# Other places for X copies, transposes, routing pieces, weight halves and the last chunks in attention

## The chip, the cores and the metric

The kernel runs on one core of a Trainium2 chip. The metric is device time in microseconds (us) from start to end of the program. Three runs of the kernel before took 641.72, 642.62 and 643.10 us (median 642.62). A fourth execution was profiled: all rows in this document come from it.

The engines are PE (TensorE, matrix products), DVE (VectorE), ACT (ScalarE), POOL (GpSimd) and SP (which issues most transfers). Each works through its own list of instructions in order; an instruction waits until those of other engines that it depends on are done, and everything behind it on its engine waits too.

## What is computed

An attention with a causal window of 128 and a bias by distance, and behind it a mixture of experts that sends each token to one of 8 experts:

```
scores = scale * q @ k.T
scores = where(mask, scores + bias, -1e9)
attn = softmax(scores)
x = (attn @ v), heads side by side           # (4608 tokens, 512)
expert_idx = argmax(x @ w_gate)
out = gate_w * (relu(x @ w1[e]) @ w2[e])     # e = expert_idx of the token
```

Batch 8, 8 heads, sequence 576, head dimension 64; experts have 1024 hidden columns. All of it is 32-bit floating point.

## The kernel before

**Attention** goes over 36 chunks of 128 queries (all 8 heads of each). The work of a chunk `ch` is cut into pieces with one-letter names. On PE: `S00 S01 S10 S11`, the scores of head groups 0 and 1 (`scores`, L196 bias and L201 products, into the PSUM tiles `s_ps[0]` and `s_ps[1]`); `T`, the transposes of the exponentials (L236, into `t_ps`); `V U W Z`, the products with v (`values`, L277, into `r_ps`); `R`, `rows` (L299), which turns the result into token rows and gate logits and writes `t_ps` again. On DVE: `N0 N1` (`peak`, L211 and L213: fold and maximum), `X` (`copy_x`, L289: `r_ps` to `xT`), `I` (`invert`, L304), `Y` (`scale_rows`, L309, reads `t_ps`; then L1365 sums the logits). On ACT: `E0 E1` (`exps`, L222, eight exponentials), `P` (`place`, L244: `t_ps` to `pT`; POOL then does four selects on it, L247 and L250).

So `t_ps` goes round: `T` writes it, `P` empties it, `R` writes it, `Y` empties it, then the next `T`. `s_ps[0]` and `s_ps[1]` go round between scores, `N` and `E`. Most chunks are paired (`super_chunks`): two chunks share one `r_ps`, so the first product `V` of a pair waits until the `X` of both chunks of the pair before is done.

**The order by hand.** `PLACES`, `places` and `END` give each piece a step (relative to 4 times its chunk) and a rank in the step. `step(s)` sorts what falls in step s by rank and emits it; each engine keeps that order for the 147 steps. A *cycle* here is four steps: one `S10 S11`, one `T`, one `S00 S01`, half a pair's products, one `R`.

Into the same table other work is woven. *Routing pieces*: after every group of 5, 6, 3 or 5 chunks (`GROUPS`), `route` finds each token's expert and rank. It is a generator; each `yield` ends a piece, and `pieces` runs the next piece of every waiting group. For the groups that begin at chunks 0, 5, 10, 15 and 21 some of the small operations are on POOL (`eng`), the rest on DVE. Piece 1 is the maximum (L567); piece 2 `mk`, `oh` and `prev` (L582 to L586); piece 3 the rank products on PE (L590 to L594) and `pick` and its sums (L596 to L608); piece 4 the gates and POOL's `p`, `c`, `big` (L626 to L636); piece 5 `lp` and `eq` (L619, L643); piece 6 `rr` (L649, two instructions); piece 7 a product on PE and its sum into `base` (L655, L657). *Weight halves*: `round_half` (ACT, L1152) and `rest_half` (POOL, L1157) split a 128 x 512 half of an expert weight into two parts; `load_half` loads it. *Q scaling* (`scale_q`, POOL, L110). *Early expert work* (`EP`): two gathered tiles are transposed (`p0`, `p1`, L791), and the first layer of expert 0 is done for the first 256 of its tokens (`0` to `6`, L834, `LE` gives those done inside `route_last`).

`requests` issues the loads on SP that are due (`paced`). After the last chunk, `route_last` finishes the routing; its `idx` lets POOL gather the other rows of expert 0 (L782). Then the **experts** run on PE almost without a gap to the end (L834 first layer, L1040 second layer).

The lines at which the order is made:

```
n, i = divmod(s - 4 * W0 - at, 4 * W1)
todo.append((HOOKS["G"], 0, lambda: pieces(lambda c: c not in PACE and s % 4 == 3)))
for _, _, f in sorted(todo, key=lambda x: x[:2]):
    f()
```

Of the kernel before, what the change touches and what calls it, by code (L numbers as in the profile page):

```python
# [52 lines left out]
def attention(ctx, tc, st, qT, kT, v, iw, load_c2, chunk_done, chunks, begun):  # L53
# [326 lines left out]
    def step(s):  # L380
# [11 lines left out]
        for name, f in (("round", 0), ("rest_of", 3)):
            at, rank = HOOKS[name]
            n, i = divmod(s - 4 * W0 - at, 4 * W1)
            if i == 0 and 0 <= n < 14:
                todo.append((rank, 0, lambda name=name, n=n: st[name](n // 2, n % 2)))
# [33 lines left out]
ASIDE = (31, 33, 35)  # L430
ASIDE_X = (33, 34)
END = {0: dict(V=(7, 1), U=(7, 3), X=(8, 0.5), R=(10, 1), I=(10, 4), Y=(11, 2)),
       1: dict(V=(10, 0.9), U=(11, 3), X=(12, 0.5), R=(14, 1), I=(14, 4), Y=(15, 2)),
       30: dict(R=(22, 2.5), I=(22, 2.6), Y=(22, 3.2)),
       31: dict(R=(19, 3), I=(19, 3.1), Y=(19, 3.2)),
       32: dict(X=(15, 1), R=(16, 3), I=(16, 3.1), Y=(16, 3.2)),
       33: dict(V=(9, 3.5), U=(9, 3.6), W=(10, 3), Z=(10, 3.1), X=(11, 1.1), R=(13, 1), I=(13, 1.1), Y=(13, 1.2)),
       34: dict(V=(8, 1), U=(8, 1.1), X=(8, 2), R=(9, 3), I=(9, 3.1), Y=(9, 3.2)),
       35: dict(T=(3, 2), P=(3, 2.5), V=(6, 1), U=(6, 1.1), X=(6, 2), R=(6, 3), I=(6, 3.1), Y=(6, 3.2))}

# [995 lines left out]
```

## Time and profile before

| what | us |
|---|---|
| median of three runs (lowest, highest) | 642.62 (641.72, 643.10) |
| the profiled execution | 641.88 |
| its span (first to last instruction) | 639.80 |
| PE busy in the span | 590.5 (92%) |
| DVE, ACT, POOL busy | 379.7, 297.1, 319.7 |

Times in all rows count from the start of the span; the profiled execution has 2.08 us around it. Busy shares are means over stages that differ: until about 215 us attention uses all four engines, behind it PE alone is near full. A wait is the idle time of an engine just ahead of an instruction, put down to what ended it.

### The profile page before, as it was taken

The page shows a single profiled execution, that of the slowest core. Times are in us where ns is not written, and L with a number is a line of the kernel's source. Part 1 is how long each engine was busy: PE and PEld are TensorE (multiplying, and loading weights), DVE is VectorE, ACT ScalarE, POOL GpSimd, SP SyncE. Part 2 cuts the span into 40 slices and gives each one's busy share as a digit, 9 for nine tenths or more (in the row PEclk, how much of TensorE's full clock was granted, in tenths as well). Part 3 has the DMA queues.
Part 4 walks back from the last instruction along what each step waited for, and adds up shares of the span by engine and source line. Part 5 has one row for each costly group of instructions (what it writes and reads, how often), then busy time and mean ns, then how long its engine had stood idle before and what let it go on. Part 6 is the DMA issues. An engine that isn't in the chain of part 4 may idle for free.

```text
span 639.8 us, 18460 instructions
## 1 busy us (share of the span) xinstructions
PE 590.5 (92%) x7406; PEld 510.0 (80%) x7406; DVE 379.7 (59%) x914; ACT 297.1 (46%) x893; POOL 319.7 (50%) x484
## 2 busy tenths in 40 slices
PE   7879788889767889999999999999999999999996
PEld 5767666767656768989889999899899998888884
DVE  3757878888968767545553564465465456356411
ACT  5978878778644214433342343334333333333311
POOL 5667968867863031066417615742760760570202
PEclk9999999999889999999999999999999999999999
DMA  7768768768442263573525325433543542544201
GB/s 246 251 201 278 228 212 248 240 207 262 137 143 76 86 202 102 183 253 109 197 92 189 111 86 174 130 99 116 170 113 103 169 123 92 176 129 135 71 1 62
DMA packets 46907, 99.23 MB, mean 155 GB/s; under 512 B 12053, under 2 KB 13077, under 8 KB 46818
## 3 DMA queue, kind: packets, MB, share of 16 engines
q1 hardware_dynamic: 38194, 76.80, 37.3%
q0 software_dynamic: 8336, 20.96, 11.4%
q8 instruction: 59, 0.97, 0.6%
q10 hardware_dynamic: 288, 0.26, 0.1%
q14 instruction: 30, 0.25, 0.1%
HBM read 77.91 MB, written 20.09 MB: 153 GB/s over the span
## 4 chain that ended last, share of the span: by engine, by line
PE 64%; DVE 1%; DMA 1%; ACT 0%; POOLq 0%; issue 0%; POOL 0%; DVEq 0%
PE y_ps L1040 31%; PE l_ps L834 30%; PE s_ps L834 1%; PE x_ps L791 1%; DMA xg<-xd,idx 1%; PE y_ps L999 1%; PE x_ps L999 0%; ACT pT L839 0%; POOLq L1204 0%; ACT e_hh L837 0%; DVE y L1048 0%; PE s_ps L299 0%; DVE xT L289 0%; ACT l_ex L703 0%; DVE e_hl L840 0%
## 5 line engine op out<-in xcount | busy, mean ns | idle before, releaser
L837 ACT ACTIVATE hh<-l_ps 128x320 fp32r<-128x320 f32 (+4 forms) x104 | 46.5, 448 | 199.3 <-PE l_ps L834 199.3
L841 DVE SCALAR_TENSOR_TENSOR hl<-l_ps,hh 128x320 fp32r<-128x320 f32 (+4 forms) x104 | 52.2, 502 | 145.8 <-ACT hh L837 145.6
L814 POOL DMA_INDIRECT xg<-xd,od_idx x112 | 118.0, 1053 | 35.0 <-issue 32.5
L222 ACT ACTIVATE pe<-s_ps,nmax 128x128 f32<-128x128 f32 x288 | 102.2, 383 | 22.8 <-DVE nmax L213 7.9
L1040 PE MATMUL y_ps<-wh,hh 128*128 128x512 f32 x280 | 109.9, 392 | 0.0
L1040 PE MATMUL y_ps<-wl,hh 128*128 128x512 f32 x280 | 109.3, 390 | 0.0
L1040 PE MATMUL y_ps<-wh,hl 128*128 128x512 f32 x280 | 109.2, 390 | 0.0
L1028 POOL DMA_INDIRECT out<-y,od_pidx x33 | 34.5, 1044 | 146.5 <-ACT y L1046 140.0
L1140 DVE TENSOR_TENSOR wl<-w_raw,wh 128x512 fp32r<-128x512 f32 x114 | 73.8, 689 | 31.5 <-ACT wh L1136 31.2
L834 PE MATMUL l_ps<-xh,wh 128*128 128x320 f32 (+8 forms) x416 | 81.0, 316 | 0.0
L834 PE MATMUL l_ps<-xl,wh 128*128 128x320 f32 (+8 forms) x416 | 80.4, 315 | 0.0
L834 PE MATMUL l_ps<-xh,wl 128*128 128x320 f32 (+8 forms) x416 | 80.3, 315 | 0.0
L834 PEld LDWEIGHTS l_ps<-xh,wh 128*128 128x128 f32 x416 | 67.8, 188 | 6.7 <-issue 1.2
L277 PE MATMUL r_ps<-pT,v_sb 64*64 64x64 f32 (+2 forms) x1728 | 58.8, 264 | 9.8 <-DVE xT L289 6.2
L834 PEld LDWEIGHTS l_ps<-xl,wh 128*128 128x128 f32 x416 | 65.9, 188 | 2.0
L834 PEld LDWEIGHTS l_ps<-xh,wl 128*128 128x128 f32 x416 | 65.8, 188 | 2.0
L222 ACT ACTIVATION_READ_ACCUMULATOR pe<-s_ps,nmax 128x1 f32 x288 | 63.6, 221 | 0.0
L201 PE MATMUL s_ps<-k_sb,q_sb 64*64 64x192 f32 (+2 forms) x1152 | 61.8, 319 | 1.1 <-issue 1.1
L1136 ACT CAST wh<-w_raw 128x1024 fp32r<-128x1024 f32 x57 | 59.5, 1044 | 5.3 <-DMA w_raw<-w 5.3
L1040 PEld LDWEIGHTS y_ps<-wh,hl 128*128 128x128 f32 x280 | 52.6, 188 | 11.5
L1040 PEld LDWEIGHTS y_ps<-wh,hh 128*128 128x128 f32 x280 | 52.6, 188 | 9.7 <-ACT hh L837 0.4
L1040 PEld LDWEIGHTS y_ps<-wl,hh 128*128 128x128 f32 x280 | 52.6, 188 | 9.1
(236 smaller groups left out, 871.7 us busy)
## 6 DMA issues: line engine op xcount, KB each, us to landing
w_raw<-w SPq DMA_DIRECT2D x56, 512.0 KB, 3.8
v_sb<-v SPq DMA_DIRECT2D x36, 256.0 KB, 3.8
xd<-x_sb SPq DMA_DIRECT2D x32, 288.0 KB, 2.7
q_sb<-qT SPq DMA_DIRECT2D x35, 256.0 KB, 3.8
k_sb<-kT SPq DMA_DIRECT2D x23, 256.0 KB, 3.3
w_raw<-w SPq DMA_DIRECT2D x16, 256.0 KB, 3.7
w_n<-w SPq DMA_DIRECT2D x4, 1024.0 KB, 5.6
k_sb<-kT SPq DMA_DIRECT2D x8, 384.0 KB, 4.0
```

The source lines that it names most:

```text
L201: anchor(nc.tensor.matmul(out=heads[half(a), c, n, 64 * u0:].rearrange("q (u x) -> q u x", x=64), lhsT=blocks["q", ch][half(c), 2 * g + n, ...
L222: nc.scalar.activation(out=pes[ch][:, 2 * g + n, :, c, :], in_=s_ps[g][:, c, 192 * n + 64:192 * n + 192].rearrange("q (u x) -> q u x", x=6 ...
L277: anchor(nc.tensor.matmul(out=tops[half(p % 2), c, p // 2, i:i + n, :], lhsT=blocks["v", j][half(c), r, p, :], rhs=diagonal(pTs[group], ha ...
L791: nc.tensor.transpose(out=x_ps[:, d, :], in_=g[:, SUB * d + E:SUB * d + E + 128], identity=st["ident"])
L814: ins = tc.nc.gpsimd.indirect_dma_start(out=g[:, s], out_offset=None, in_=parts, in_offset=bass.IndirectOffsetOnAxis(ap=idx[:, s], axis=0),)
L834: nc.tensor.matmul(out=ps, lhsT=a[:, 128 * d:128 * d + 128], rhs=b[:, d], start=(k == 0), stop=(k == 11))
L837: nc.scalar.activation(out=hh, in_=ps, func=AF.Relu)
L841: nc.vector.scalar_tensor_tensor(out=hl, in0=ps, scalar=0.0, in1=hh.bitcast(F32), op0=ALU.max, op1=ALU.subtract)
L1028: ins = nc.gpsimd.indirect_dma_start(**kw).ins
L1040: nc.tensor.matmul(out=ys[t], lhsT=a[:, tl], rhs=b[:, 512:1024], start=(f == 0 and k == 0), stop=(f == 7 and k == 2))
L1136: keep(tc, nc.scalar.copy(out=wh, in_=raw))
L1140: keep(tc, eng.tensor_tensor(out=wl[:, sl], in0=raw[:, sl], in1=wh.bitcast(F32)[:, sl], op=ALU.subtract))
```

## The change

The places are other numbers. In words:

- `X` of the first chunk of a pair goes from the start of step 20 to the end of step 19; `X` of the second from behind `N1` of the running chunk to ahead of it (rank 2.5 to 0.3). `V` of a second chunk goes from step 10 (ahead of `R`) to step 11 (behind `R`, next to `U`).
- `T` goes from the end of step 4 to the start of step 5, `N0` behind `I`, `W` of some chunks ahead of `T` and `Z` behind it.
- Routing pieces run at the start of every third step of a cycle, ahead of `R`, `E1`, `I` and `N0`; before, they ran in the fourth step, ahead of `Y`. `prev` is on DVE in every group.
- Weight halves come every 9 steps from step 22 to 139 (before: every 8, from 20 to 124), at varying ranks. The loads get due times to match, and no load is placed later than step 148 (before: 140). Q is scaled one step earlier.
- The last chunks (30 to 35) have new places; `X` of chunk 32 goes to ACT too. Both early transposes `p0 p1` run in step 142, first layer `3` in step 146, `4 5` ahead of the last rank, `6` behind the last index products (before: `3 4`, then `5 6` between rank and index products).

```diff
-        if ch in ASIDE_X:
+        if ch in X_ACT:
...
-        at = min(due, PN * 35)
+        at = min(due, PN * 37)
...
-        ahead.setdefault(max(0, 4 * ch - 11), []).append(ch)
+        ahead.setdefault(max(0, 4 * ch - QAT[0]), []).append(ch)
...
-        todo.append((HOOKS["G"], 0, lambda: pieces(lambda c: c not in PACE and s % 4 == 3)))
+        for m, rank in PIECES:
+            if s % 4 == m:
+                todo.append((rank, 0, lambda: pieces(lambda c: c not in PACE)))
...
-PLACES = dict(S10=(0, 1), S11=(0, 2), E0=(0, 3), T=(4, 4), N1=(1, 2), P=(5, 3), S00=(-3, 5), S01=(-3, 6),
-              R=(22, 1), E1=(2, 2), N0=(-2, 3), I=(22, 4), Y=(23, 2))
+PLACES = {'S10': (0, 1), 'S11': (0, 2), 'E0': (0, 3), 'T': (5, 0.7), 'N1': (1, 2), 'P': (5, 3), 'S00': (-3, 5), 'S01': (-3, 6), 'R': (22, 1), 'E1': (2, 2), 'N0': (-2, 8), 'I': (22, 4), 'Y': (23, 2)}
...
+FIRST = {'X': (19, 5.5)}
+SECOND = {'V': (11, 2.5), 'U': (11, 3), 'W': (14, 0.9), 'Z': (15, 3), 'X': (17, 0.3)}
...
+PIECES = ((2, 0.5),)
...
-        at.update(X=(20, 0.5))
...
-        at.update(V=(10, 0.9), U=(11, 3), W=(14, 0.9), Z=(15, 3), X=(17, 2.5))
...
-EP = {0: ((30, "z"),), 52: ((30, "o"),), 131: ((30, "g"),), 142: ((2.3, "p0"),), 143: ((3.5, "p1"),), 144: ((2.5, "0"),), 145: ((2, "1"),), 146: ((2.5, "2"),)}
-LE = ("34", "56", "")
+EP = {0: ((30, 'z'),), 52: ((30, 'o'),), 131: ((30, 'g'),), 146: ((2.5, '2'), (3.53, '3')), 144: ((3.3, '0'),), 142: ((8, 'p0'), (8, 'p1')), 145: ((5.5, '1'),)}
+LE = ('45', '', '6')
...
-    eng.tensor_copy(out=prev, in_=run[:, c0, :])
+    nc.vector.tensor_copy(out=prev, in_=run[:, c0, :])
```

Three places in the instruction lists show what moved. The changed file is 11 lines shorter there, so L1365 reads L1354, L649 reads L638 and so on.

On DVE, around chunks 11 and 12, before: `Y` and its sum (L309, L1365), `X` (L289), `N1` (L211, L213), the second `X`, `N0`, `I` (L304), pieces 7 and 2 of two groups, then the next `Y`.

```order
L309 TENSOR_TENSOR x_sb<-t_ps,rinv 128x576
L1365 TENSOR_REDUCE lg<-x_sb 128x8
L289 COPY xT<-r_ps 128x512
L211 COPY_PREDICATED s_ps<-mask_sb,s_ps 128x2x2x64
L213 TENSOR_REDUCE nmax<-s_ps 128x4
L289 COPY xT<-r_ps 128x512
L211 COPY_PREDICATED s_ps<-mask_sb,s_ps 128x2x2x64
L213 TENSOR_REDUCE nmax<-s_ps 128x4
L304 RECIPROCAL rinv<-rsum 128x8
L657 TENSOR_TENSOR base<-base,s_ps 128x48
L582 TENSOR_REDUCE mk<-key 128x5
L584 TENSOR_TENSOR oh<-key,mk 128x40
```

The same place of the changed kernel:

```order
L309 TENSOR_TENSOR x_sb<-t_ps,rinv 128x576
L1354 TENSOR_REDUCE lg<-x_sb 128x8
L289 COPY xT<-r_ps 128x512 x2
L211 COPY_PREDICATED s_ps<-mask_sb,s_ps 128x2x2x64
L213 TENSOR_REDUCE nmax<-s_ps 128x4
L646 TENSOR_TENSOR base<-base,s_ps 128x48
L571 TENSOR_REDUCE mk<-key 128x5
L573 TENSOR_TENSOR oh<-key,mk 128x40
L575 CAST prev<-run 128x8
L304 RECIPROCAL rinv<-rsum 128x8
L211 COPY_PREDICATED s_ps<-mask_sb,s_ps 128x2x2x64
L213 TENSOR_REDUCE nmax<-s_ps 128x4
```

Both `X` now stand ahead of `N1`, and the pieces stand between `N1` and `N0` instead of between `N0` and `Y`.

On PE, the end of `S00 S01`, then `V` of chunk 10, `R` of chunk 7 and `U`, before:

```order
L201 MATMUL s_ps<-k_sb,q_sb 64x192 x8
L277 MATMUL r_ps<-pT,v_sb 64x128 x8
L277 MATMUL r_ps<-pT,v_sb 64x64 x8
L299 MATMUL t_ps<-iw_sb,xT 64x72 x16
L277 MATMUL r_ps<-pT,v_sb 64x128 x8
L277 MATMUL r_ps<-pT,v_sb 64x64 x8
```

And changed:

```order
L201 MATMUL s_ps<-k_sb,q_sb 64x192 x8
L299 MATMUL t_ps<-iw_sb,xT 64x72 x16
L277 MATMUL r_ps<-pT,v_sb 64x128 x8
L277 MATMUL r_ps<-pT,v_sb 64x64 x8
L277 MATMUL r_ps<-pT,v_sb 64x128 x8
L277 MATMUL r_ps<-pT,v_sb 64x64 x8
```

`R` now runs ahead of `V`, which is the instruction that waits for the two `X`.

On PE, the last routing (L710, L711 the rank of the last chunk, L834 the first layer, three rows each for `4`, `5` and `6`, L655 the first of the index products), before:

```order
L834 MATMUL s_ps<-e_xl,wh 128x256 x4
L710 LDWEIGHTS tri
L710 MATMUL t_ps<-l_oh,tri 128x8
L711 LDWEIGHTS tri
L711 MATMUL t_ps<-l_prev,tri 128x8
L834 MATMUL s_ps<-e_xh,wh 128x256 x4
L834 MATMUL s_ps<-e_xh,wl 128x256 x4
L834 MATMUL s_ps<-e_xl,wh 128x256 x4
L834 MATMUL s_ps<-e_xh,wh 128x256 x4
L834 MATMUL s_ps<-e_xh,wl 128x256 x4
L834 MATMUL s_ps<-e_xl,wh 128x256 x4
L655 LDWEIGHTS lp
```

And changed (L823 is the first layer, L699 and L700 the rank, L644 the index products):

```order
L823 MATMUL s_ps<-e_xh,wh 128x256 x4
L823 MATMUL s_ps<-e_xh,wl 128x256 x4
L823 MATMUL s_ps<-e_xl,wh 128x256 x4
L699 LDWEIGHTS tri
L699 MATMUL t_ps<-l_oh,tri 128x8
L700 LDWEIGHTS tri
L700 MATMUL t_ps<-l_prev,tri 128x8
L644 LDWEIGHTS lp
L644 MATMUL s_ps<-rr,lp 128x48
```

The index products now follow the rank directly; the first layer `6` stands behind them.

## Rows read from the trace of the kernel before

**Rows 1.** Busy time by stage: stretch, length, PE, PEld, DVE, ACT, POOL, clock, DMA.

```profile
29.20:166.20 137.00, 114.73 (x3498) 93.97 (x3496) 107.38 (x245) 108.84 (x464) 103.82 (x201) 1.00 0.73 230
166.20:215.20 49.00, 38.54 (x1049) 32.57 (x1049) 37.76 (x105) 22.62 (x89) 23.76 (x47) 0.93 0.39 118
215.20:239.30 24.10, 20.25 (x171) 16.39 (x172) 16.92 (x89) 5.79 (x16) 5.62 (x6) 1.00 0.51 148
239.30:639.80 400.50, 394.46 (x2226) 350.08 (x2225) 201.11 (x441) 139.26 (x235) 168.67 (x184) 1.00 0.41 128
```

**Rows 2.** Who waited for whom, 29.2 to 166.2: us in total, times, longest.

```profile
DVE s_ps L211 <- PE s_ps L201: 15.5, 12, 2.5
...
PE s_ps L196 <- ACT pe L222: 4.8, 8, 1.8
PE t_ps L236 <- DVE x_sb L309: 4.7, 5, 2.1
PE r_ps L277 <- DVE xT L289: 4.3, 6, 0.9
...
PE r_ps L277 <- POOL pT L247: 1.0, 1, 1.0
```

**Rows 3.** Timeline around a `V` behind two `X`: start, us, instruction, idle before.

```profile
112.53 0.68 DVE L289 COPY xT<-r_ps 128x512 f32<-128x512 f32 x1
...
113.13 0.42 DVE L211 COPY_PREDICATED s_ps<-mask_sb,s_ps 128x256 f32<-128x256 uint32 x1
...
114.19 0.68 DVE L289 COPY xT<-r_ps 128x512 f32<-128x512 f32 x1
...
114.97 0.96 PE L277 MATMUL r_ps<-pT,v_sb 64*64 64x192 f32 x13 [0.96 <-POOL pT L247]
```

**Rows 4.** Timeline around a piece ahead of `Y`.

```profile
104.40 0.77 DVE L619 TENSOR_TENSOR lp<-c_sb,p 128x640 bf16<-128x640 f32 x1
...
105.78 0.80 DVE L643 TENSOR_TENSOR eq<-c_sb,c 128x240 f32<-128x240 f32 x1 [0.60 <-POOL c L636]
...
106.50 0.74 DVE L309 TENSOR_TENSOR x_sb<-t_ps,rinv 128x576 f32<-128x576 f32 x1
...
107.30 0.71 PE L236 MATMUL t_ps<-c_sb,pe 64*128 64x64 f32 x16 [1.06 <-DVE x_sb L309]
```

**Rows 5.** Two transposes with a cycle between them.

```profile
118.54 0.71 PE L236 MATMUL t_ps<-c_sb,pe 64*128 64x64 f32 x16 [0.39 <-DVE x_sb L309]
...
122.62 0.71 PE L236 MATMUL t_ps<-c_sb,pe 64*128 64x64 f32 x16
```

**Rows 6.** PE's waits, 166.2 to 215.2.

```profile
PE t_ps L236 <- DVE x_sb L309: 3.5, 2, 2.2
PE s_ps L591 <- POOL prev L586: 2.3, 1, 2.3
PE r_ps L277 <- DVE xT L289: 1.9, 1, 1.9
PE s_ps L299 <- DVE base L657: 1.4, 1, 1.4
```

**Rows 7.** Busy time of four us behind the wait for `prev`.

```profile
178.00:182.00 4.00, 3.93 (x62) 2.91 (x65) 1.86 (x8) 1.51 (x8) 2.23 (x6) 0.58 0.10 33
```

**Rows 8.** Timeline of the last routing and the gather behind it.

```profile
222.83 0.87 DVE L728 TENSOR_SCALAR l_lp<-c_sb,rank 128x128 bf16<-128x128 f32 x4
...
226.69 0.42 PE L655 MATMUL s_ps<-rr,lp 128*128 128x48 bf16 x10
...
228.43 1.17 POOL L782 DMA_INDIRECT xg<-xd,idx  x1 [21.67 <-DVE e_hl L840]
...
232.24 0.65 PE L791 MATMUL x_ps<-c_sb,xg 128*128 128x128 f32 x4 [1.15 <-DMA xg<-xd,idx]
```

**Rows 9.** One line's instructions: ns least/median/most, for `rr` on DVE.

```profile
L649 DVE TENSOR_TENSOR rr<-eq,c_sb x14: 295/588/900, 84.5 to 222.0; 128x240 bf16<-128x240 f32 x8, 128x288 bf16<-128x288 f32 x4, 128x144 bf16<-128x144 f32 x2
```

**Rows 10.** The same for a select on POOL.

```profile
L247 POOL TENSOR_SCALAR_AFFINE_SELECT pT<-pT x56: 651/657/760, 18.7 to 204.7; 64x512 f32<-64x512 f32 x56
```

More of the change, by code (lines that the diff above doesn't have):

```diff
@@ L331, in attention @@
     for n in range(16):
-        wanted.append((PN * (W0 + W1 * n) - LEAD[3], PN * (W0 + W1 * (n - 2 * WR)) + 3 if n >= 2 * WR else 0, st["load_half"], (n // 2, n % 2)))
+        m = 2 * (n // 2)
+        first = REST[m - 5][0] + 1 if m >= 2 * WR else 0
+        wanted.append((max(first, PN * ((ROUND[m][0] if m < 14 else 140) // 4) - LEAD[3]) + 2 * (n % 2), first, st["load_half"], (n // 2, n % 2)))
     paced = {}
@@ L386, in step @@
         todo = [(rank, ch, lambda k=k, ch=ch: do(k, ch)) for rank, ch, k in plan.get(s, ())]
-        todo += [(HOOKS["Q"], n, lambda ch=ch: scale_q(nc.gpsimd, ch)) for n, ch in enumerate(ahead.get(s, ()))]
+        todo += [(QAT[1], n, lambda ch=ch: scale_q(nc.gpsimd, ch)) for n, ch in enumerate(ahead.get(s, ()))]
         if s < len(WU) - 1:
             todo.append((19, 0, lambda: warm_up(WU[s + 1])))
-        todo.append((HOOKS["G"], 0, lambda: pieces(lambda c: c not in PACE and s % 4 == 3)))
+        for m, rank in PIECES:
+            if s % 4 == m:
+                todo.append((rank, 0, lambda: pieces(lambda c: c not in PACE)))
         todo.append((20, 1, lambda: pieces(lambda c: s in PACE.get(c, ()))))
[L392 to L396, printed above, removed]
+        for name, at in (("round", ROUND), ("rest_of", REST)):
+            todo += [(rank, n, lambda name=name, n=n: st[name](n // 2, n % 2)) for n, (k, rank) in enumerate(at) if k == s]
         todo += [(rank, 9, lambda op=op: early(op)) for rank, op in EP.get(s, ())]
@@ L413, in attention @@
         step(s)
-PLACES = dict(S10=(0, 1), S11=(0, 2), E0=(0, 3), T=(4, 4), N1=(1, 2), P=(5, 3), S00=(-3, 5), S01=(-3, 6),
-              R=(22, 1), E1=(2, 2), N0=(-2, 3), I=(22, 4), Y=(23, 2))
-HOOKS = dict(Q=7, G=1.5, round=(0, 3.5), rest_of=(2, 21))
+PLACES = {'S10': (0, 1), 'S11': (0, 2), 'E0': (0, 3), 'T': (5, 0.7), 'N1': (1, 2), 'P': (5, 3), 'S00': (-3, 5), 'S01': (-3, 6), 'R': (22, 1), 'E1': (2, 2), 'N0': (-2, 8), 'I': (22, 4), 'Y': (23, 2)}
+ALONE = {'V': (14, 0.9), 'U': (15, 3), 'X': (16, 0.5)}
+FIRST = {'X': (19, 5.5)}
+SECOND = {'V': (11, 2.5), 'U': (11, 3), 'W': (14, 0.9), 'Z': (15, 3), 'X': (17, 0.3)}
+BEFORE_ALONE = {'V': (10, 2.5), 'U': (11, 1.8), 'W': (12, 4.5), 'Z': (13, 3.3), 'X': (17, 0.3)}
+QAT = (12, 8)
+PIECES = ((2, 0.5),)
+ROUND = [(22, 4.3), (31, 4.3), (40, 4.3), (49, 4.3), (58, 4.3), (67, 4.3), (76, 4.3), (85, 4.3), (94, 4.3), (103, 4.3), (112, 4.3), (121, 4.3), (130, 4.3), (139, 4.3)]
+REST = [(23, 0.7), (32, 0.7), (41, 0.7), (50, 0.7), (59, 0.7), (68, 0.7), (77, 0.7), (86, 0.7), (95, 0.7), (104, 0.7), (113, 0.7), (122, 0.7), (131, 0.7), (140, 0.7)]
+X_ACT = (32, 33, 34)
+ASIDE = (31, 33, 35)
+END = {0: {'V': (7, 1), 'U': (7, 3), 'X': (8, 0.5), 'R': (10, 1), 'I': (10, 4), 'Y': (11, 2)}, 1: {'V': (10, 0.9), 'U': (11, 3), 'X': (12, 0.5), 'R': (14, 1), 'I': (14, 4), 'Y': (15, 2)}, 30: {'R': (22, 2.5), 'I': (21, 2.5), 'Y': (22, 3.2), 'W': (11, 3.3)}, 31: {'R': (19, 3), 'I': (18, 3.7), 'Y': (19, 3.2), 'V': (15, 1.8)}, 32: {'X': (15, 1), 'R': (16, 3), 'I': (15, 0.7), 'Y': (16, 3.2)}, 33: {'V': (9, 3.5), 'U': (9, 3.6), 'W': (9, 6.5), 'Z': (10, 3.1), 'X': (11, 1.1), 'R': (13, 1), 'I': (13, 1.1), 'Y': (13, 1.2)}, 34: {'V': (8, 1), 'U': (8, 1.1), 'X': (8, 2), 'R': (9, 3), 'I': (9, 3.1), 'Y': (9, 3.2), 'S10': (-1, 3.3)}, 35: {'T': (3, 2), 'P': (3, 2.5), 'V': (6, 1), 'U': (6, 1.1), 'X': (6, 2.2), 'R': (6, 3), 'I': (6, 3.1), 'Y': (6, 3.2)}}
 SLOTS = dict(S11=0, T=1, S01=2, V=3, W=3)
@@ L424 @@
 SOON = 10
-W0 = 5
-W1 = 2
 TW = 320
[L430 to L439, printed above, removed]
 def super_chunks(n):
@@ L452, in places @@
     group = next(g for g in super_chunks(N // 128) if ch in g)
-    if len(group) == 1:
-        at.update(V=(14, 0.9), U=(15, 3), X=(16, 0.5))
-    elif ch == group[0]:
-        at.update(X=(20, 0.5))
-    else:
-        at.update(V=(10, 0.9), U=(11, 3), W=(14, 0.9), Z=(15, 3), X=(17, 2.5))
-        if (ch + 1,) in super_chunks(N // 128):
-            at.update(W=(12, 4.5), Z=(12, 4.6))
+    at.update(ALONE if len(group) == 1 else FIRST if ch == group[0] else BEFORE_ALONE if (ch + 1,) in super_chunks(N // 128) else SECOND)
     if ch == 0:
@@ L497 @@
 APART_TO = 27
-PACE = {21: (128, 130, 131, 133, 135, 137, 139), 27: (140, 141, 142, 143, 144), 30: (145, 146)}
+PACE = {21: (128, 130, 131, 133, 135, 137, 139), 27: (140, 141, 142, 143, 145), 30: (145, 146)}
+EP = {0: ((30, 'z'),), 52: ((30, 'o'),), 131: ((30, 'g'),), 146: ((2.5, '2'), (3.53, '3')), 144: ((3.3, '0'),), 142: ((8, 'p0'), (8, 'p1')), 145: ((5.5, '1'),)}
+LE = ('45', '', '6')
 GROUPS = ((0, 5), (5, 5), (10, 5), (15, 6), (21, 6), (27, 3), (30, 5), (35, 1))
```

## The prediction

> **What bounds the kernel now.** I read first the busy time by stage [rows 1]. From 239.3 us on PE is busy 394.46 of 400.50 us: the experts run at PE's pace, none of their code changes, so whatever ends attention earlier moves this block forward by as much. Ahead of it the time is shared: from 29.2 to 166.2 us (26 cycles, from the transpose of chunk 4 to that of chunk 30) PE is busy 114.73 us of 137.00, DVE 107.38, ACT 108.84 and POOL 103.82. No engine is full; each waits for the others in turn. PE is nearest to it, and its idle time, 22.27 us here, 10.46 us from 166.2 to 215.2 and 3.85 us from there to the experts, 36.6 us in all, is what an order alone can win. Then I read who waited for whom [rows 2, 6], and for each wait the places in the timeline [rows 3, 4, 8].
>
> What a cycle takes when nothing waits is seen in [rows 5]: 122.62 - 118.54 = 4.08 us from one `T` to the next, against 137.00 / 26 = 5.27 us in the mean.
>
> **The change part by part**, against the profiled execution's 641.88 us.
>
> *`V` behind two `X`.* In [rows 3] DVE does `X`, then `N1`, then the second `X` from 114.19 to 114.87; PE's `V` starts at 114.97 after 0.96 us idle. The view names POOL, but it starts right behind DVE's `X`, so I count it here. With the rows that name `xT`, 4.3 and 1.0 us [rows 2], that is 5.3 us in this stage. Changed, the second `X` runs one `N1` (1.06 us, 113.13 to 114.19) earlier, and `V` one `R` later. A wait of at most 0.96 us is then covered twice: all 5.3 us go. What is late next is `N1`, now behind both `X`, and with it `E1`; what hides that is ACT, which still has `E0` and `P` to do. Bounds: 0 to -5.3, and below in the rivals.
>
> *Pieces ahead of `N0` instead of ahead of `Y`.* In [rows 4] piece 5 fills DVE from 104.40 to 106.50 (0.60 us of it waiting for POOL), `Y` follows, and `T` starts 1.06 us late. Such waits of `T` are 4.7 us [rows 2]. The work stays on DVE, and `Y` still comes after it; but DVE sat idle for 15.5 us ahead of its `N` because the scores weren't there yet [rows 2], and the piece now starts in that gap. A long piece (2.1 us) doesn't fit one gap (15.5 / 12 = 1.3 us), a short one does. I take half: -2.4, bounds 0 and -4.7. Waits of scores for ACT (4.8 us) I leave as they are: nothing in the exponentials changes.
>
> *`T`, `W`, `Z`, Q, weight halves.* `T` moves past no other PE work except a `W` in four places; `W` then runs while `T` would wait. Q is scaled a step earlier on POOL, which has 33 us free in this stage [rows 1]. The fourteen halves are the same ones, over 119 steps instead of 106; ACT and POOL carry 1 of 9 steps' worth less here and pay it behind step 124, where ACT is busy 22.62 of 49.00 us and POOL 23.76 [rows 1]. Their loads move with them on SP's queue; at a DMA share of 0.73 [rows 1] there is room. All this I put at nothing. A half's cast may now fall between `N0` and `E0` where it did not, or no longer does: one wait of scores for ACT is 4.8 / 8 = 0.6 us [rows 2]; four more would be +2.4, two fewer -1.2, and these are the bounds.
>
> *`prev` on DVE.* One wait: PE 2.3 us for POOL's `prev` [rows 6], which sat behind POOL's selects. It goes. On DVE it is one short instruction for each of five groups, in the gap above. Behind that wait the granted clock was 0.58 in the mean over 178 to 182 us [rows 7], so partly at the lower of its two levels, 1.2 instead of 2.4 GHz, after PE had stood still: 3.93 us busy x 0.42 = 1.6 us more than at full clock. Another dip comes behind the wait of 2.2 us for `Y` [rows 6], which stands ahead of piece 5 of the group that also corrects its counts; that piece is as long as before and I expect it to stay.
>
> *New end.* `V` of chunk 31 waits 1.9 us for `xT` and `R` of chunk 33 1.4 us for `base` [rows 6]. Both `X` come earlier, and `base` now follows `R` of 33 and 34: both go. With `prev` (2.3) and the clock (1.6) that makes 7.2 us of the 10.5 idle plus the dip. But DVE is busy 37.76 of 49.00 us here, ACT gets one more `X`, a weight half falls into the last cycles, and both early transposes now come in one step ahead of chunk 35's. I keep 2 us for what is late next: -5.2, bounds +2 and -9.
>
> *Last routing.* In [rows 8] DVE's last masks are done at 223.70, but the index products start at 226.69, because PE does `5` and `6` first; the gather starts at 228.43 and its rows are used at 232.24. Changed, `3` runs ahead of the rank, `6` behind the index products, while the gather is under way. The products can start about when the masks are done, 3.0 us earlier; the gather and all behind it follow. PE's idle time here is 3.85 us [rows 1], and that is the most it can give: -3.0, bounds 0 and -3.9.
>
> Sum: -5.3 - 2.4 + 0 - 5.2 - 3.0 = -15.9; 641.88 - 15.9 = 626.0. The median of the runs lies 0.74 us above the profiled execution: **626.7, say 626.5 us**.
>
> A second look at DVE and POOL. One and the same `rr` takes 295 to 900 ns on DVE, with 588 as the median [rows 9]: DVE is slowed when POOL works, and pieces move to where POOL does its selects (657 ns each [rows 10]). The Trainium skill, "SBUF — State Buffer", section "SBUF: two separate sides", says that VectorE, reading two operands from SBUF, and a GpSimd instruction that reads SBUF take one shared pair of ports in turn, whichever comes first holding it for its whole instruction. By that rule the pieces' two-operand steps would each stand behind a select; the trace agrees in part, since 900 - 295 = 605 ns is about one select, while the median is less than half of one. This is the first rival.
>
> **The rivals.**
>
> *The pieces get longer (18%).* Five groups, each with `oh`, `eq` and two `rr`: 20 instructions that could each wait one select, 20 x 0.657 = 13.1 us. Already paid: ten `rr` x (588 - 295) ns = 2.9 us. If all of the rest comes on the path, -15.9 + 10.2 = -5.7, 636.9 us. For it: the spread of `rr`. Against it: the pieces stood beside selects before too.
>
> *Almost nothing waits (15%).* If taking waits away lets the loop settle near the 4.08 us cycle, more goes than I counted: two thirds of all 36.6 us of idle PE, -24.4 us, 618 us. For it: every engine is under 80% busy from 29 to 166 except PE. Against: pieces and `Y` still make some cycles full on DVE.
>
> *Slower: `N` is late (12%).* `N1` is late by one `X` wherever a pair's copies stand ahead of it, and `N0` by a whole piece; ACT's exponentials wait, then the next scores, which need `s_ps` free. There are 13 pairs; one `X` is 0.60 us start to start (112.53 to 113.13), so 7.8 us. The pieces ahead of `N0` are mostly `lp` 0.77, `eq` 0.80 [rows 4] and two `rr` of 0.59 us [rows 9], 2.75 us for each of five groups, 13.7 us. It decides when more than 15.9 of these 21.5 us are on the path; all of them give +5.6: 648 us. For it: scores already wait 4.8 us for ACT's exponentials [rows 2]. Against: DVE's 15.5 us of idle time ahead of its `N`.
>
> *It cancels (5%).* The waits change names, the last routing's gain goes on a new stall of the experts' first weights: 642 us.
>
> **How the numbers follow.** The forecast has 50%, with its own range 620 to 633; the rivals have 18, 15, 12 and 5. 612 to 641 us leaves out the slower case, part of the cancelled one and a little below 612. Faster by over 0.2% (1.3 us, what a measurement of this kernel tells from no change): 0.50 + 0.18 + 0.15 = 0.83, less 0.01 for a worse port: 0.82. Within 0.2%: the cancelled case, 0.05. Slower: 0.13.
>
> **What would show it.** Right: in the changed profile PE no longer waits for `xT` ahead of `V`; its waits of `T` for `Y` are down by about half; the wait for `prev` is gone; the gather starts within 2 us of the last masks; the first expert product starts some 16 us earlier, near 223 us, and the block behind it still takes 400 us. Wrong: exponentials that wait for `nmax` by more than a few us in all (the slower rival), `rr` with a median near 0.9 us (the first), an expert block that got longer, or waits of POOL's Q scaling or PE's scores for DMA, which would mean that the loads moved too late.

## The result and the profile after

The changed kernel takes **628.17 us** in the median of 4 runs (627.88 to 628.57), the kernel before 642.86 us beside it (4 runs, 641.72 to 644.34): ratio **0.9771, 95% interval 0.9749 to 0.9792**, so 14.7 us less. The forecast was 626.5. The profiled execution took 628.57 us, its span 626.4 against 639.8.

I cut the span at the same events as before: the transpose of chunk 4, that of chunk 30, the last `R` of attention (L299), the experts' first product (L823). From the busy time by stretch of the kernel after (columns as in [rows 1]: length, PE, PEld, DVE, ACT, POOL, clock, DMA share, GB/s):

```profile
29.09:159.88 130.79, 114.42 (x3498) 94.08 (x3496) 107.41 (x250) 107.27 (x457) 103.69 (x198) 1.00 0.74 237
159.88:202.71 42.83, 37.60 (x1046) 32.04 (x1046) 36.23 (x105) 25.13 (x97) 24.36 (x45) 0.92 0.45 141
202.71:225.62 22.91, 20.60 (x171) 16.03 (x170) 17.82 (x94) 5.97 (x16) 5.81 (x6) 1.00 0.54 166
225.62:626.40 400.78, 394.76 (x2227) 350.29 (x2226) 200.13 (x434) 139.21 (x235) 168.59 (x183) 1.00 0.39 127
```

Cut at its own events (29.15, 166.25, 215.17 and 239.12 us) the kernel before has 137.10, 48.92, 23.95 and 400.68 us there. The three stages of attention lost 6.3, 6.1 and 1.0 us, and the experts' block kept its length. PE's busy time hardly moved (114.7 to 114.4 us in the first stage); what went is idle time (22.3 to 16.4 us there).

The waits of the first stage (who waited for whom: us, times, longest), to be read against [rows 2]:

```profile
ACT pe L222 <- DVE nmax L213: 10.8, 12, 3.4
DVE s_ps L211 <- PE s_ps L201: 7.2, 11, 1.8
PE s_ps L196 <- ACT pe L222: 5.1, 11, 1.8
PE t_ps L236 <- DVE x_sb L309: 2.2, 3, 1.5
PE t_ps L299 <- ACT pT L244: 2.0, 7, 0.5
```

The row `PE r_ps <- DVE xT` (4.3) is gone, and the transposes' waits for `Y` went from 4.7 to 2.2 us. In their place ACT's exponentials wait 10.8 us for `nmax` (0.5 before, 3 times), and PE's `R` waits 2.0 us for ACT's copy of `pT` (0.7 before). DVE's own idle time ahead of the masks halved, 15.5 to 7.2: DVE is now the later of the two.

A single row of such a view scatters from execution to execution. In five profiles with this order in the first stage (the changed kernel twice, v0, g1, g2) the transposes' waits for `Y` come to 2.2 to 5.7 us and the exponentials' for `nmax` to 8.0 to 11.7. What all five share is that no row `PE r_ps <- DVE xT` stands there, and that PE is idle for 16.4 to 18.7 us in all.

PE's waits from 159.88 to 202.71 us, against [rows 6]:

```profile
PE t_ps L236 <- DVE x_sb L309: 3.2, 2, 2.9
PE s_ps L644 <- DVE nmax L213: 2.1, 1, 2.1
PE r_ps L277 <- DVE xT L289: 0.9, 1, 0.9
```

The waits for `prev` (2.3) and `base` (1.4) are gone and that for `xT` is halved; a new one of 2.1 us stands at the index products of a group (L644). Around the two longest, in four stretches (columns as in the first view):

```profile
158.00:160.00 2.00, 0.12 (x4) 0.12 (x4) 1.93 (x6) 0.72 (x5) 1.92 (x4) 1.00 0.00 0
160.00:164.00 4.00, 4.00 (x96) 3.88 (x100) 2.70 (x7) 3.81 (x20) 2.42 (x5) 0.57 0.66 209
178.00:184.00 6.00, 2.97 (x144) 2.71 (x137) 5.90 (x13) 2.01 (x9) 4.50 (x7) 0.99 0.43 144
184.00:188.00 4.00, 4.00 (x75) 2.83 (x68) 2.59 (x10) 3.84 (x18) 1.07 (x2) 0.59 0.40 139
```

PE all but stands still from 158 to 160 us and is half idle from 178 to 184, with DVE full beside it (1.93 of 2.00, 5.90 of 6.00); behind each stop the granted clock is 0.57 to 0.59, so partly at 1.2 instead of 2.4 GHz. The kernel before had two such dips as well ([rows 7] is one). The dip that I wanted gone moved.

The last routing, from the timeline (start, us, instruction, idle before), against [rows 8]:

```profile
208.53 0.42 SPq L973 DMA_DIRECT2D w_n<-w  x1
209.00 0.49 SPq L673 DMA_DIRECT2D xd<-gate  x1
...
210.95 0.87 DVE L717 TENSOR_SCALAR l_lp<-c_sb,rank 128x128 bf16<-128x128 f32 x4
...
212.26 0.17 DVE L730 CAST idx<-base 128x16 uint32<-128x16 f32 x1
...
215.12 1.07 POOL L771 DMA_INDIRECT xg<-xd,idx  x1 [19.17 <-DVE i_n L1007]
...
218.80 0.66 PE L780 MATMUL x_ps<-c_sb,xg 128*128 128x128 f32 x4 [1.26 <-DMA xg<-xd,idx]
```

The indices follow the masks by 0.6 us, as wished. But the gather starts 2.69 us behind them (215.12 - 212.43), where it was 0.68 before (227.75 to 228.43). The view names `i_n`, which the gather doesn't read; something else holds it.

### The profile page after: what moved, and what is told of

Read it like the earlier page. It is cut to its first block, busy times and chain, and to the rows that moved or that the text cites. A ratio compares the mean times of both kernels' runs of the same rounds, so it can differ in the third digit from the quotient of the medians.

```text
span 626.4 us, 18476 instructions
## 1 busy us (share of the span) xinstructions
PE 589.8 (94%) x7406; PEld 509.1 (81%) x7406; DVE 378.1 (60%) x918; ACT 298.1 (48%) x894; POOL 320.9 (51%) x479
## 4 chain that ended last, share of the span: by engine, by line
PE 77%; ACT 7%; POOL 6%; DVE 6%; issue 2%; DMA 2%; POOLq 0%; SPq 0%; ACTq 0%; DVEq 0%
PE y_ps L1029 31%; PE l_ps L823 30%; PE r_ps L277 4%; PE s_ps L201 3%; ACT pe L222 3%; ACT pT L244 3%; PE t_ps L236 2%; POOL pT L247 2%; POOL pT L250 2%; PE s_ps L823 2%; PE t_ps L299 2%; PE s_ps L196 1%; DMA w_raw<-w 1%; DVE nmax L213 1%; PE y_ps L988 1%
## 5 line engine op out<-in xcount | busy, mean ns | idle before, releaser
L222 ACT ACTIVATE pe<-s_ps,nmax 128x128 f32<-128x128 f32 x288 | 102.0, 377 | 23.6 <-DVE nmax L213 19.8
L823 PE MATMUL l_ps<-xh,wh 128*128 128x320 f32 (+8 forms) x416 | 81.1, 316 | 0.0
L823 PE MATMUL l_ps<-xl,wh 128*128 128x320 f32 (+8 forms) x416 | 80.4, 315 | 0.0
L823 PE MATMUL l_ps<-xh,wl 128*128 128x320 f32 (+8 forms) x416 | 80.3, 315 | 0.0
L823 PEld LDWEIGHTS l_ps<-xh,wh 128*128 128x128 f32 x416 | 67.7, 188 | 7.2 <-issue 1.2
L823 PEld LDWEIGHTS l_ps<-xl,wh 128*128 128x128 f32 x416 | 65.9, 188 | 2.0
L823 PEld LDWEIGHTS l_ps<-xh,wl 128*128 128x128 f32 x416 | 65.8, 188 | 2.0
L222 ACT ACTIVATION_READ_ACCUMULATOR pe<-s_ps,nmax 128x1 f32 x288 | 61.9, 215 | 0.0
L1029 PEld LDWEIGHTS y_ps<-wh,hl 128*128 128x128 f32 x280 | 52.6, 188 | 11.4
L277 PE MATMUL r_ps<-pT,v_sb 64*64 64x64 f32 (+2 forms) x1728 | 56.1, 264 | 3.0 <-issue 2.1
```

Of the source, the lines that this page charges most:

```text
L222: nc.scalar.activation(out=pes[ch][:, 2 * g + n, :, c, :], in_=s_ps[g][:, c, 192 * n + 64:192 * n + 192].rearrange("q (u x) -> q u x", x=6 ...
L277: anchor(nc.tensor.matmul(out=tops[half(p % 2), c, p // 2, i:i + n, :], lhsT=blocks["v", j][half(c), r, p, :], rhs=diagonal(pTs[group], ha ...
L823: nc.tensor.matmul(out=ps, lhsT=a[:, 128 * d:128 * d + 128], rhs=b[:, d], start=(k == 0), stop=(k == 11))
L1029: nc.tensor.matmul(out=ys[t], lhsT=a[:, tl], rhs=b[:, 512:1024], start=(f == 0 and k == 0), stop=(f == 7 and k == 2))
```

## The experiments

Twelve runs, on several chips whose times for the kernel before differ by up to 4 us; so the ratio to the kernel before, run beside each, is what is compared. The stage lengths are of one profiled execution each. The first stage of the changed kernel is 130.8 to 133.4 us in five profiles that share it (the changed kernel twice, v0, g1, g2; v0 differs in `prev` alone), and that of the kernel before 137.1, or 140.1 in e1: a difference under 3 us there says little. PE's idle time in it (its length less PE's busy time) leaves out what the clock does: 16.4 to 18.7 us in those five, 22.3 in the kernel before and 23.9 in e1.

| run | base and edit | ratio (95%) | first stage | PE idle in it | second | last `R` to experts |
|---|---|---|---|---|---|---|
| x1 | before + X, V | 0.9994 (0.9971 to 1.0017) | 139.2 | 24.1 | 48.9 | 23.9 |
| p1 | before + pieces | 0.9953 (0.9927 to 0.9978) | 136.5 | 19.8 | 48.6 | 23.9 |
| xp | before + both | 0.9934 (0.9911 to 0.9957) | 134.0 | 19.8 | 49.8 | 24.0 |
| e1 | before + new end | 0.9890 (0.9857 to 0.9924) | 140.1 | 23.9 | 43.1 | 24.0 |
| a0 | after, again | 0.9784 (0.9759 to 0.9810) | 132.0 | 17.2 | 41.8 | 23.7 |
| y0 | after, old X, V | 0.9824 (0.9786 to 0.9863) | 132.8 | 17.5 | 43.3 | 23.5 |
| r0 | after, old halves | 0.9774 (0.9744 to 0.9804) | 131.6 | 17.5 | 42.8 | 23.8 |
| v0 | after, prev on POOL | 0.9759 (0.9736 to 0.9782) | 132.2 | 18.1 | 41.6 | 24.1 |
| l1 | after, two long pieces later | 0.9764 (0.9733 to 0.9795) | 132.4 | 18.0 | 42.1 | 22.6 |
| g1 | after, w_n later | 0.9791 (0.9755 to 0.9826) | 133.4 | 17.7 | 42.3 | 25.2 |
| g2 | after, w_n later still | **0.9722 (0.9697 to 0.9747)** | 132.6 | 18.7 | 42.3 | **21.6** |
| b1 | g2, V ahead of R | 0.9743 (0.9711 to 0.9776) | 135.0 | 18.2 | 42.6 | 21.5 |

**x1: X and V alone.**

```diff
-        at.update(X=(20, 0.5))
+        at.update(X=(19, 5.5))
-        at.update(V=(10, 0.9), U=(11, 3), W=(14, 0.9), Z=(15, 3), X=(17, 2.5))
+        at.update(V=(11, 2.5), U=(11, 3), W=(14, 0.9), Z=(15, 3), X=(17, 0.3))
-            at.update(W=(12, 4.5), Z=(12, 4.6))
+            at.update(V=(10, 2.5), U=(11, 1.8), W=(12, 4.5), Z=(12, 4.6))
```

> The kernel before with the places of X and V of the change alone: both X of a pair ahead of N1, V behind R and Y; nothing else moves. My theory (the wait of V for the second X is what it removes): PE no longer waits for xT ahead of V in the first stage (5.3 us before), the stage from the transpose of chunk 4 to that of chunk 30 goes from 137.1 to 132 us, the time by -5.3 us, to about 637.5. Rival (N1 is late behind both X): the waits of ACT for nmax, 0.5 us before, grow to 5 us or more, the stage keeps 135 us or more, the time is 641 or above.

No change. The wait that the edit aims at is gone, the row `PE r_ps <- DVE xT` no longer stands in the waits of the first stage, and others took its place:

```profile
PE t_ps L236 <- DVE x_sb L309: 6.5, 6, 2.0
...
ACT pe L222 <- DVE nmax L213: 5.3, 8, 0.8
PE s_ps L196 <- ACT pe L222: 4.1, 6, 1.8
PE t_ps L299 <- ACT pT L244: 3.7, 12, 0.5
...
PE s_ps L590 <- DVE nmax L213: 2.1, 2, 1.1
PE s_ps L655 <- DVE nmax L213: 1.7, 2, 1.0
```

Before, `T`'s waits for `Y` were 4.7 us, the exponentials' for `nmax` 0.5 and `R`'s for `pT` 0.7; rows of routing products (L590, L655) that wait for `nmax` did not stand in this stage. `N1` is late behind both `X`, and `V` no longer stands in front of `R`. The late `N1` reached PE by the routing products and not by the scores, whose wait for the exponentials was 4.8 us before and is 4.1 here. PE is idle for 24.1 us, not less than before. The rival was right for this edit by itself.

**p1: the pieces alone.**

`N0` goes behind `I` with them, as in the change.

```diff
-s % 4 == 3)))
+s % 4 == 2)))
-N0=(-2, 3)
+N0=(-2, 8)
-HOOKS = dict(Q=7, G=1.5,
+HOOKS = dict(Q=7, G=0.5,
```

> The kernel before with the routing pieces alone moved: ahead of N0 (step 2 of the cycle) and no longer ahead of Y. My theory: the waits of the transposes for Y, 4.7 us in the first stage, are about halved, the stage is 2.4 us shorter, the time about 640.4. Rival (N0 late behind a whole piece): the exponentials wait for nmax for 5 us or more where it was 0.5, and the time is the same or longer, 643 to 648.

-3.0 us (0.0047 x 642.86; -1.4 to -4.7), the size that was forecast, but not by the wait that was forecast. The waits of the first stage:

```profile
ACT pe L222 <- DVE nmax L213: 14.6, 11, 3.2
...
PE s_ps L196 <- ACT pe L222: 6.3, 15, 1.8
PE t_ps L236 <- DVE x_sb L309: 4.5, 4, 2.0
...
PE r_ps L277 <- DVE xT L289: 2.1, 5, 0.6
```

The transposes' waits for `Y`, which were to be halved, stay at 4.5 us (4.7 before). The rival's sign came, exponentials that wait 14.6 us for `nmax`, and the time fell all the same. The last row is what counts: moving the pieces alone halves `V`'s wait for `xT` (4.3 to 2.1).

**xp: both.** The edits of x1 and p1 together.

> The kernel before with both moves of the cycle: X and V (alone they gave nothing) and the pieces ahead of N0 (alone -0.5%). Theory of interaction: X and V alone only handed PE's wait for xT on to other waits, since DVE's order was full ahead of Y and N1; with the pieces gone from ahead of Y the room is there, and both together give more than the sum, 6 us (ratio 0.990), the first stage at 131 to 132 us as in the changed kernel. Rival: what shortened the first stage is the weight halves, which are spread wider in the changed kernel; then the two moves together give what the pieces gave alone, about -3 us (ratio 0.995), the stage stays at 134.5 us or more.

-4.2 us (-2.8 to -5.7), more than the pieces alone by 1.2 us, which the intervals don't separate; not the 6 us of my theory. The first stage of the kernel before, x1, p1 and xp (columns as in [rows 1]):

```profile
29.15:166.25 137.10, 114.78 (x3500) 94.02 (x3498) 107.40 (x246) 108.89 (x464) 103.91 (x202) 1.00 0.73 230
29.05:168.23 139.18, 115.07 (x3500) 95.28 (x3498) 107.49 (x246) 108.78 (x464) 103.89 (x202) 0.99 0.71 225
28.99:165.49 136.50, 116.72 (x3498) 97.23 (x3497) 106.73 (x246) 106.82 (x458) 104.34 (x201) 0.97 0.73 231
28.78:162.81 134.03, 114.22 (x3499) 95.15 (x3498) 105.08 (x246) 107.16 (x458) 103.31 (x200) 1.00 0.74 233
```

PE's idle time is 19.8 us in p1 and in xp alike: `X` and `V` take nothing more away here. That p1's stage is 2.5 us longer is PE's busy time, at a granted clock of 0.97 for 1.00. In the second stage, which is untouched, PE still waits as in [rows 6]:

```profile
PE s_ps L591 <- POOL prev L586: 2.9, 1, 2.9
...
PE s_ps L299 <- DVE base L657: 1.4, 1, 1.4
```

**y0: the changed kernel with X and V at their old places.** The edit is x1's, undone (`FIRST`, `SECOND`, `BEFORE_ALONE`, for `X` and `V`).

> The changed kernel with X and V of the pairs back at their old places (second X behind N1, V ahead of R). Theory from the runs so far (that move alone gave nothing, and 1 us when the pieces are moved too): the same within 1.5 us of the changed kernel, ratio 0.977 to 0.981, with PE's waits for xT ahead of V back (2 to 5 us) and the exponentials' waits for nmax (10.8 us in the changed kernel) down by about as much. Rival, the prediction's own term: the move is worth 5.3 us in the company of the rest, ratio 0.985 or above.

631.94 us, 0.0040 over a0, which ran on another chip. On its own chip all six of its runs (630.47 to 636.89 us) lie above the six of r0 (629.20 to 629.99), the changed kernel but for its halves: 2.5 us between the medians. The row of its first stage:

```profile
PE r_ps L277 <- DVE xT L289: 0.4, 1, 0.4
```

By this row `V` hardly waits, but the row misleads. As in [rows 3], other waits of `V` have another name, and `V` still starts right behind the second `X`. One of them, and one of the kernel before:

```profile
99.94 0.68 DVE L289 COPY xT<-r_ps 128x512 f32<-128x512 f32 x1
...
100.77 0.90 PE L277 MATMUL r_ps<-pT,v_sb 64*64 64x128 f32 x32 [0.74 <-POOL c L625]
```

```profile
65.67 0.68 DVE L289 COPY xT<-r_ps 128x512 f32<-128x512 f32 x1
...
66.45 0.88 PE L277 MATMUL r_ps<-pT,v_sb 64*64 64x192 f32 x16 [0.91 <-issue]
```

In the timeline of the first stage, PE's waits ahead of `V` that end within 0.15 us of the end of a second `X` come to 7.0 us in the kernel before (nine), 2.4 in p1 (six) and 3.1 here (seven); x1, xp and the changed kernel have none. So the theory's sign, 2 to 5 us of these waits, came; the exponentials' waits for `nmax` did not go down (11.4 us), while `R`'s for `pT` fell to 0.7. In the profiled execution, the fastest of the six, PE is idle for 17.5 us of the first stage, no more than in profiles of the changed kernel (16.4 to 18.7), so the trace doesn't show where the 2.5 us of the medians go. In size they are less than half of the prediction's 5.3.

**r0: the weight halves back on their raster.**

```diff
-ROUND = [(22, 4.3), (31, 4.3), (40, 4.3), ...]
-REST = [(23, 0.7), (32, 0.7), (41, 0.7), ...]
+ROUND = [(20 + 8 * n, 3.5) for n in range(14)]
+REST = [(22 + 8 * n, 21) for n in range(14)]
```

> The changed kernel with the weight halves back on the old raster (every eight steps from 20, behind E0). The first stage takes 134.0 us with both moves of the cycle on the kernel before, and 130.8 to 132.0 in the changed kernel; what is left between them is the halves, Q and the place of T. Theory: it is the halves (two of them, 1.3 us of ACT and 2.5 of POOL, leave the stage, and the rest stand behind N0 instead of between E0 and P): the stage is back at 133.5 to 134.5, the ratio at 0.981 to 0.983. Rival: it is Q or T: the stage keeps 131 to 132 and the ratio 0.977 to 0.979.

The same as the changed kernel: the halves are worth nothing that these runs show, as the prediction had it, and my theory of the first runs falls. The rival named Q and `T`. No run moves either of them alone, so they stay untested.

**e1: the new end alone.** `END`, `X_ACT`, the one paced piece and `prev` of the change, in the kernel before; early products and last routing stay.

> The kernel before with the new end of attention alone (places of chunks 30 to 35, X of chunk 32 on ACT, one paced piece a step later, prev on DVE); cycle, halves, early products and last routing as before. Theory (the prediction's term, -5.2): waits for xT (1.9), base (1.4) and prev (2.3) between 166 and 215 us go, that stage from 48.9 to 42.5 to 44 us, ratio 0.990 to 0.992. Rival: in the changed kernel it was the earlier cycle and the halves that made the end shorter; alone it gives less than 2 us, ratio 0.997 or above.

-7.1 us (-4.9 to -9.2). The second stage is 43.1 us as in the changed kernel (48.9 before), so the new end stands on its own:

```profile
169.14:212.26 43.12, 35.41 (x1045) 29.60 (x1045) 36.92 (x105) 23.16 (x89) 24.51 (x46) 1.00 0.44 134
```

Of these 5.8 us, 2.7 are idle time of PE (10.42 to 7.71) and 3.1 are busy time (38.50 to 35.41), at a granted clock of 1.00 for 0.93. The clock of this stage scatters: 0.90 to 0.97 in the four profiles with the old end, 0.92 to 1.00 in the ten with the new. PE's idle time in it doesn't mix: 10.4 to 11.7 us with the old end, 4.9 to 7.7 with the new.

**v0: prev back on POOL.**

```diff
-    nc.vector.tensor_copy(out=prev, in_=run[:, c0, :])
+    eng.tensor_copy(out=prev, in_=run[:, c0, :])
```

> The changed kernel with the copy to prev back on POOL for the groups that route on POOL. Theory (the prediction's term): the wait of PE for prev, 2.3 us behind POOL's selects around 178 us, and the clock behind it (1.6 us) come back: +2 to +4 us against the changed kernel, 630 to 632 by its first times. Rival: in the changed kernel PE stands still there for the scores' maxima anyway (L644, 2.1 us at 183 us), prev is hidden and the time is the same within 1 us.

No loss. The wait is 0.3 us in the new end, with the copy on POOL (PE's waits, second stage):

```profile
PE s_ps L644 <- DVE nmax L213: 1.9, 1, 1.9
...
PE s_ps L580 <- POOL prev L575: 0.3, 1, 0.3
```

So the new order is enough to take the 2.3 us away, without the copy on DVE. Whether the copy on DVE would be enough in the old order, no run shows.

**l1: two long pieces behind N0.**

```diff
-                todo.append((rank, 0, lambda: pieces(lambda c: c not in PACE)))
+                todo.append((8.5 if s == 122 else rank, 0, lambda: pieces(lambda c: c not in PACE)))
-PACE = {21: (128, 130, 131, 133, 135, 137, 139), ...
+PACE = {21: (128, 130, 131, 133, 135, 139, 141), ...
```

> The changed kernel, with two long routing pieces put behind the N0 that they stand ahead of: the one that corrects the counts (lp, the correction, eq: 154.1 to 158.0 us on DVE) and the two rr at 180.0 to 181.6. Theory: N0 behind these pieces leaves the exponentials and then PE idle (2.9 us ahead of the transpose at 159.9, and 179 to 184 us), and the clock falls behind both stops; behind N0 they cost less: -2 to -5 us, 623 to 626. Rival: the pieces then stand ahead of Y, and the transposes wait for that instead, as they did in the kernel before (2.2 us there): within 1 us of 628.2.

The same within the noise, as the rival said: from 155 to 205 us the transposes wait 3.7 us for `Y`, 3 times (3.2 us, twice, in the changed kernel), and a dip of the clock stands at 178 to 182 us (0.57). Where these two pieces stand made no difference to the time.

**g1 and g2: the load in front of the last gate store.** In g1 the load waits for the last routing's index products, in g2 for the first gathered rows to be turned:

```diff
 (g1, in route_last)
-            nc.tensor.matmul(out=ip[:, E * t:E * t + E], ...)
+            st["quiet"] = nc.tensor.matmul(out=ip[:, E * t:E * t + E], ...).ins
 (g2)
-            behind(tc, r, st["quiet"])
+            behind(tc, r, st["seen"][2])     # the first x_ps transpose of the experts
```

> The changed kernel, with the first load of w_n (sent at 208.53 us, just ahead of the last gate store at 209.00) held back until the last routing's index products. Theory: the first gather, at 215.12 us, waits for the gate store to land, and that lies behind the load on the DMA engines (5.1 us to landing); without the load in front the store lands in some 2 us, the gather starts within 1 us of the indices (about 213), the experts' first product at 223.3 to 224.3 instead of 225.6, the time is 626 to 627.2 (-1 to -2). Rival: the gather waits for something of DVE (the rows name i_n, 214.88): it starts at 215.1 as before and the time stays at 628.2.

> The changed kernel with the first load of w_n held until the first gathered rows are turned on PE, so that it runs neither ahead of the last gate store nor beside the first gathers (beside them, in the run before, the first rows came 5.8 us behind the gather's start and not 3.7). Theory: gather at 0.7 us behind the indices, first rows used 2 us earlier than in the changed kernel, experts 1 to 1.3 us earlier: -1 us. Rival: the load, now behind two weight loads, comes late for the narrow tile of the first expert or slows the weights around 243 to 251 us, and the gain is lost there: 0 to +2 us.

From the transfers of the changed kernel (size of one, us to landing): first a gate store sent at 206.2, ahead of the load, then the load (208.53) and the last gate store behind it (209.00):

```profile
xd<-gate SPq DMA_DIRECT2D x1, 0.5 KB, 1.4
```

```profile
w_n<-w SPq DMA_DIRECT2D x1, 1024.0 KB, 5.4
xd<-gate SPq DMA_DIRECT2D x1, 0.5 KB, 5.1
```

With a load in front, five profiles have the last store's landing: 4.9 to 5.6 us. For g1 and g2 the views don't have it.

In g1 the gather starts 0.68 us behind the indices (214.36 to 215.04), so the load was what held it: shown, and `i_n` (216.81 in g1) is out. That it did so by way of the store is argued: the gather reads what the store writes, and in three profiles (the changed kernel twice, r0) it starts 1.0 to 1.1 us behind the store's landing. But in g1 the load runs beside the gather, and its rows are used 5.84 us behind its start (3.68 in the changed kernel):

```profile
220.88 0.76 PE L780 MATMUL x_ps<-c_sb,xg 128*128 128x128 f32 x4 [3.20 <-DMA xg<-xd,idx]
```

PE stands still for 3.2 us, and the products behind it take 0.63 us instead of 0.39: the dip again (granted clock 0.57 from 220.88 to 224.00). The gain was given back. In g2 the load comes at 218.89, the gather 0.69 us behind the indices (213.64) and its rows 3.83 us later:

```profile
214.33 1.17 POOL L771 DMA_INDIRECT xg<-xd,idx  x1 [17.49 <-DVE e_hl L830]
...
218.16 0.66 PE L780 MATMUL x_ps<-c_sb,xg 128*128 128x128 f32 x4 [1.20 <-DMA xg<-xd,idx]
```

That 1.2 us is PE's only wait from the last `R` to the experts, a stretch of 21.6 us (22.9 and 23.7 in two profiles of the changed kernel). On the same chip g2 takes 626.45 us and the changed kernel 629.66, with ratios whose intervals don't overlap: the fastest kernel here.

**b1: V ahead of R again, both X early, on g2.**

> The fastest kernel so far (the changed kernel with the first load of w_n behind the first gathered rows, 0.972 of the kernel before), with V of the pairs ahead of R again while both X stay ahead of N1. Theory: R of the changed kernel waits 2.0 us in the first stage for ACT's copy of pT, which V ahead of it used to cover (0.7 us); with the X early, V finds xT copied (at most 0.5 us of waits), so 1.3 us go, ratio 0.970. Rival: PE's order isn't what limits the cycle any more, DVE's maxima and ACT's exponentials are (10.8 us of waits for nmax): the wait turns up there, the same within 1 us, 0.971 to 0.974.

As the rival has it: 0.9743, not faster than g2. `R`'s wait for `pT` is back to 0.7 us, and in the first stage the exponentials wait 12.9 us for `nmax` (8.0 in g2).

**a0, the changed kernel once more.**

> The changed kernel once more, on the chip that runs the three kernels beside it, so that they can be compared with it: 0.977 of the kernel before, as at first (0.975 to 0.979).

It came out at 0.9784, 0.001 above the first measurement.

## Why the prediction was right, and where it was not

The time, 628.2 for 626.5, lies in the range. The general mechanism held: idle time went, busy time hardly changed, and what ended earlier ahead of the experts was gained in full, since their block kept its length. That the sum came so near is in part luck: two terms were too large (`X` and `V`, last routing), one perhaps too small (the end), and one came by another wait than the one it was priced from (the pieces). By the steps:

*V behind two X: -5.3. This step failed.* "A wait of at most 0.96 us is then covered twice: all 5.3 us go." The wait went and the time stayed (x1). Two things were wrong. The price wasn't nothing: `N1` behind both `X` and `R` without `V` in front cost as much as was won, and of ACT I had written that it still had work to do. And the same idle time can be taken by another term: with the pieces away from `Y`, most of this wait goes by itself (7.0 us to 2.4 in p1, counted by the timeline; the 5.3 us left out two waits that the view puts down to "issue").

*Pieces: -2.4. The size was right, the wait was not.* -3.0 alone, inside its bounds, and 2.5 us of PE's idle time; but the transposes' waits for `Y` stayed, 4.5 us in p1 and 6.5 in xp, and what went was `V`'s wait, which I had counted in the step above. The agreement in size is luck. The two terms together, -7.7, measured -4.2 (-2.8 to -5.7). The slower rival's mechanism, `N` late, is in every run with these moves (exponentials waiting 5 to 15 us), and the time fell all the same: PE's own wait for the exponentials went from 4.8 us only to 6.3 and 6.1 (p1, xp) and 5.1 (the changed kernel).

*T, Q, halves: 0.* Right for the halves (r0). For `T` and Q it is open: from xp to the changed kernel PE's idle time in the first stage falls from 19.8 us to between 16.4 and 18.7, and no run moves `T` or Q by itself.

*New end: -5.2.* -7.1 alone (-4.9 to -9.2), and 5.8 to 7.3 us in that stage: at least what was forecast. PE's idle time there fell from 10.42 to 5.23 us (48.92 - 38.50, 42.83 - 37.60). The 1.6 us of the clock are not shown: 0.92 against 0.93 in the first pair of profiles, and it scatters in the others (e1). And `prev` went by the order, with the copy on either engine (v0).

*Last routing: -3.0. Failed in its second half.* "The products can start about when the masks are done, 3.0 us earlier; the gather and all behind it follow." The products did, and the gather did not: 3.30 us behind the last masks (211.82 to 215.12), where I asked for 2. It also reads the gate column of the rows, and the last gate store lay behind the load of `w_n` on the way to memory. The kernel before sends load and store in the same order, but its indices come 5.85 us behind the store's start (221.90 to 227.75) and not 3.43. In e1 and xp, which keep its last routing, the store landed 5.0 and 5.6 us behind its start (219.00 and 219.16), 0.9 and 0.4 us ahead of the indices (224.86 and 225.21), so nothing waited for it. 1.0 us came of this step in the first pair of profiles, 0.2 in a0; with the load out of the way 2.4 (23.95 to 21.58). The Trainium skill, "DMA: Bandwidth & Descriptors", section "Queues, rings and completion order", says that a DMA's semaphore lands only after every earlier write of the same DMA engine. The changed kernel agrees: 5.1 us behind the load, 1.4 for a store of the same size ahead of it.

*The rivals.* "The pieces get longer" is out: `rr` has a median of 406 ns in the changed kernel, not 588 or more. "Almost nothing waits" is out too: PE is still idle for 16.4 us in the first stage. The cancelling stall of the experts' weights didn't come: their block took 400.78 us for 400.68. Their first product starts at 225.6 us, 13.5 earlier and not 16.

Taken apart, both moves of the cycle (-4.2), the end (-7.1) and the tail (about -1) make -12.3 of the 13.9 to 14.7 us. The rest, 1.6 to 2.4 us, is within what these intervals leave open, and `T` and Q may have a part in it. What `X` and `V` are worth in company is open as well: nothing in xp's idle time, some 2.5 us by y0 against r0.

## What to carry to other kernels

Waits of one engine on several lines of another are one budget, and the name that a view gives a wait can be another's: count a wait by the instruction that ends just before it does. So, before adding up what two reorderings give, ask whether the first already moves the producer of the second, and price what the moved instruction now stands in front of. A step that is shortened ends at the next of its inputs, and that can be a transfer that was in time by a few tenths of a us and showed in no view: list what the waiting instruction reads, and when each landed. A small store that something waits for goes ahead of a large load in the queue, not behind it; and the load doesn't belong beside the gather that follows either (g1).
